# A fused attention and two-layer kernel: four buffers for the even batches' m, and other half-blocks for its four parts

## The chip, the cores and the metric

One NeuronCore of one Trainium2 chip. The metric is the device time of one execution in microseconds (us), over several runs. Matmuls run on the tensor engine (PE), elementwise work on VectorE (DVE), ScalarE (ACT) and GpSimd (POOL); the transfers are issued from SyncE's queue (SP).

## The reference, cut to what matters

```python
# x: [8, 8, 512, 64], state: [8, 8, 32, 64]; heads are joined to 512 columns
a = softmax(x @ state.T / 8)          # each of 512 tokens over 32 states
xread = a @ state
a2 = softmax(state @ x.T / 8)         # each state over 512 tokens
sread = a2 @ x
x = concat([xread, sread])            # 8 batches of 544 tokens, 512 wide
h = relu(x @ w_in)                    # 1024 wide
c = conv3(h)                          # three taps along the tokens, per column
y = (h * sigmoid(c)) @ w_out
xk = mu_k * y + (1 - mu_k) * previous(y)
xr = mu_r * y + (1 - mu_r) * previous(y)
out = sigmoid(xr @ w_r) * (relu(xk @ w_k) ** 2 @ w_v)
```

## The kernel before, in words

Everything runs in float32, with each operand of a large product split into a high and a low part (`fp32r`), and three matmuls (high by high, high by low, low by high) in the place of one (`mm3`).

The first phase works through nine tiles t: t = 0 to 7 are the 512 tokens of batch t, t = 8 the states of all batches. Each tile has eight steps f of 128 hidden columns. A step computes `hps` (the hidden columns before the relu), `hb` (after it), `cacc` (the convolution: one ACT and two DVE instructions), `g` (sigmoid on ACT, product on DVE), `gs` (split into high and low), and `acc`, twelve matmuls of 512 columns with w_out. The second phase does the last three lines of the reference for nine tiles of 512 tokens.

For the tokens the hidden layer isn't computed from xread. The state is multiplied with w_in first: m = state @ w_in, and then `hps` = m.T @ a, six matmuls a step (three for each group g of four heads). m has four parts q for each batch; part q serves the steps f = 2q and 2q + 1. For batches 2 to 7 the products for an even batch and the odd one behind it are made together by `pair_m(b, q, g)`: six matmuls of 256 columns for each of two head groups into one PSUM bank, an eviction (high part on ACT, low part on DVE), and eight transfers for a part, four of which go into the even batch's tile `me` and four into the odd one's `m_odd`. `m_odd` has room for four parts, `me` for two: part q goes into buffer q % 2.

The attention of the next batch is computed beside a batch's steps: scores `p_s`, maxima, exp (`e2`, `q`), norms and transpositions (`aT`, then the split copy `aring` that `hps` reads), transpositions on PE (`p_a2`, copied to `a2T`), the products `p_sr` with x, and their transpositions `p_srT`. Scores, `p_m`, `p_a2`, `p_sr` and `p_srT` share a ring of two PSUM banks (tag "at"). A bank is handed on in the order of the code, when its last reader is done.

What stands where is set in half-blocks: each step f of a tile has two, and batch b begins at half-block 16 b. `M_PARTS` gives for each part the half-block, counted from the batch's first, in which it is emitted; its second head group follows one half-block later. Each emission also has a priority, and a scheduler sets from priorities and readiness the order in which each engine gets its instructions. That order is fixed in the built program: each engine and the SP queue take their instructions strictly in turn.

Of the kernel before, what the change touches and what calls it, by code (L numbers as in the profile page):

```python
# [8 lines left out]
F32 = mybir.dt.float32  # L9
F32R = mybir.dt.float32r  # L10
# [16 lines left out]

ATTEND = 3
M_PARTS = (-8, -4, 3, 8)


@with_exitstack
def tile_kernel(
# [27 lines left out]
    B, P, NST, H, D = x_n.shape  # L61
    KC, S = x_t.shape[1], x_t.shape[3]
    NS = st_bd.shape[2] // (2 * KC)
    KF = w_in.shape[0]
    DM = H * D
    G = H * NS // P
# [117 lines left out]
    def load_s(b, ap):  # L184
        sT[b] = ap.tile([P, KC, 2, NS], F32, tag="sT", name="sT", bufs=3)
        nc.sync.dma_start(out=sT[b].rearrange("p c u n -> p (c u n)"), in_=st_bd[b])

    def load_t(b, ap):
        xT[b] = ap.tile([P, KC, S], F32, tag="xT", name="xT", bufs=1)
        for c in range(KC):  # L190
            nc.sync.dma_start(out=xT[b][:, c], in_=x_t[b, c])

    def load_n(b, ap):
        xn[b] = ap.tile([P, NST, H, D], F32, tag="xn", name="xn", bufs=1)
        nc.sync.dma_start(out=xn[b], in_=x_n[b])

    def m_of(b, q):

        if b % 2:
            return m_odd[:, q]  # L200
        if not m_even:
            m_even.extend(ap.tile([P, 2, G, 2 * P], F32R, tag=f"me{i}", name=f"me{i}") for i in range(2))
        return m_even[q % 2]

    def pair_state(b):

        bd = bds[:, (b // 2 + 1) % 2]
        for i in range(2):
            sb = sT[b + i].rearrange("p c u n -> p c (u n)")
            n = slice(2 * NS * i, 2 * NS * (i + 1))  # L210
            nc.scalar.activation(bd[:, 0, :, n], sb, AF.Copy)
            nc.gpsimd.tensor_tensor(bd[:, 1, :, n], sb, bd[:, 0, :, n].bitcast(F32), op=ALU.subtract)

    def pair_m(b, q, g):

        bd, w = bds[:, (b // 2 + 1) % 2], W["in", "group", q // 2]
        fs = slice(q % 2 * 2, q % 2 * 2 + 2)  # L220
        p = ps_a.tile([P, 512], F32, tag="at", name="p_m")
        for i in range(2):
            c = 2 * g + i
            o = p[:, 2 * P * i:2 * P * (i + 1)].rearrange("p (f c) -> p f c", c=P)
            mm3(o, [(bd[:, 0, c], bd[:, 1, c])], [[w[:, l, fs, c * P:(c + 1) * P] for l in range(2)]], True, True)
        tag = ("raw", "mid")[g]
        r = stg.tile([P, 2, 2, 2 * P], F32R, tag=tag, name="m", bufs=STAGED[tag])
        src = p.rearrange("p (i n) -> p i n", i=2)
        nc.scalar.activation(r[:, 0], src, AF.Copy)
        nc.vector.tensor_tensor(r[:, 1], src, r[:, 0].bitcast(F32), op=ALU.subtract)  # L230
        for j, rj in HALF:
            for i, ri in HALF:
                nc.sync.dma_start(out=m_of(b + j, q)[ri, :, g].bitcast(F32), in_=r[rj, :, i].bitcast(F32))

    class Attention:
# [20 lines left out]
        def m(self, q, f0, n):  # L256

            w = W["in", "group", q // 2]
            fs = slice(q % 2 * 2 + f0, q % 2 * 2 + f0 + n)
            sl = slice(f0 * P, (f0 + n) * P)  # L260
            p = self.at("p_m").rearrange("p (g f c) -> p g f c", g=G, c=P)[:, :, :n]
            for g in range(G):
                cs = (2 * g, 2 * g + 1)
                mm3(
                    p[:, g], [(self.bd[:, 0, c], self.bd[:, 1, c]) for c in cs],
                    [[w[:, l, fs, c * P:(c + 1) * P] for l in range(2)] for c in cs], True, True,
                )
            src = p.rearrange("p g f c -> p g (f c)")
            if self.b == 0:
                nc.scalar.activation(m_first[q // 2][:, q % 2, :, sl], src, AF.Copy)  # L270
                return
            d = m_of(self.b, q)
            nc.scalar.activation(d[:, 0, :, sl], src, AF.Copy)
            nc.vector.tensor_tensor(d[:, 1, :, sl], src, d[:, 0, :, sl].bitcast(F32), op=ALU.subtract)
# [134 lines left out]
    def g1_main(t, f):  # L409
        p = ps_h.tile([P, 512], F32, tag="h", name="hps")  # L410
        if t < B:
            sl = slice(f % 2 * P, f % 2 * P + P)
            if t == 0:
                m = m_first[f // 4][:, f // 2 % 2]
                for g in range(G):
                    nc.tensor.matmul(p, m[:, g, sl], a_first[:, g], start=g == 0, stop=g == G - 1)
                st1[t, f] = {"p": p}
                return
            m, a = m_of(t, f // 2), aring[:, t % 2]
            mm3(  # L420
                p, [(m[:, 0, g, sl], m[:, 1, g, sl]) for g in range(G)],
                [(a[:, 0, g], a[:, 1, g]) for g in range(G)], True, True,
            )
        else:
            v = xs.rearrange("p l c b n -> p l c (b n)")
            mm3(
                p[:, :B * NS], [up(W["in", f], k) for k in range(KC)],
                [(v[:, 0, k], v[:, 1, k]) for k in range(KC)], True, True,
            )
        st1[t, f] = {"p": p}  # L430
# [177 lines left out]
    ap = ap_cm.__enter__()  # L608

    m_first = [ap.tile([P, 2, G, 2 * P], F32, tag=f"me{i}", name=f"mf{i}") for i in range(2)]  # L610
    a_first = ap.tile([P, G, S], F32, tag="af", name="a_first")
    m_even = []
    half = {}

    def at_half(k, *fns, prio=None):
        p = 500 * k - AHEAD if prio is None else prio
        half.setdefault(k, []).extend((fn, p) for fn in fns)
# [51 lines left out]
    def attend(b, k, first):  # L669

        a_ = a if first else Attention(b, ap)
        if not first:
            at_half(k, a_.begin, a_.scores)
            if b == 1:
                at_half(M_PARTS[0] + 2 * KF - 1, a_.state)
            at_half(k + 1, lambda: a_.max1(0, nc.vector), lambda: a_.max1(1, nc.gpsimd))
            at_half(k + 2, lambda: a_.max2(0), lambda: a_.max2(1), a_.neg2)
            at_half(k + 3, a_.exps, prio=500 * k - EXP_AHEAD)
            if b + 1 < B:
                at_half(k + 3, lambda: load_t(b + 1, ap))  # L680
            if b % 2 and b + 1 < B:
                at_half(k + 3, lambda: load_s(b + 1, ap), lambda: load_s(b + 2, ap))
            h = 2 * KF * b
            for q, d in enumerate(M_PARTS):
                if b == 1:
                    at_half(h + d, lambda q=q: a_.m(q, 0, 2), prio=500 * (h + d) - M_AHEAD)
                elif b % 2 == 0:
                    if q == 0:
                        at_half(h + d - 1, lambda: pair_state(b))
                    for g in range(G):  # L690
                        at_half(h + d + g, lambda q=q, g=g: pair_m(b, q, g), prio=500 * (h + d + g) - M_AHEAD)
            at_half(k + 4, lambda: a_.norm1(0, nc.vector))
            at_half(k + 5, lambda: a_.norm1(1, nc.gpsimd))
            at_half(k + 6, lambda: a_.turn1(0))
            at_half(k + 7, lambda: a_.turn1(1))
            k += 9
        at_half(k, a_.norm2, lambda: a_.turn2(0))
        at_half(k + 1, lambda: a_.turn2(1))
        at_half(k + 2, a_.sread)
        if b + 1 < B:  # L700
            at_half(k + 2, lambda: load_n(b + 1, ap))
        at_half(k + 3, a_.sturn)
# [15 lines left out]
    at_half(0, lambda: load_s(1, ap), lambda: load_t(1, ap), prio=-500)  # L718
    at_half(0, lambda: load_n(0, ap), prio=0)
    attend(0, 1, True)  # L720
    for b in range(1, B):
        attend(b, (b - 1) * H1 + ATTEND, False)
# [6 lines left out]
    for i in range(len(slots) + 2):  # L729
        if i < len(slots):  # L730
            ph, t, f = slots[i]
# [98 lines left out]
```

## Time and profile before

| | |
|---|---|
| median of 3 runs | 889.49 us (888.82 to 893.3) |
| profiled execution | 893.46 us, its span 891.6 us |
| PE busy | 853.2 us (96%), 4394 matmuls |
| DVE busy | 546.2 us (61%) |
| ACT busy | 545.1 us (61%) |
| POOL busy | 107.7 us (12%) |

Shares of busy time are means over phases: the first phase fills roughly 80 to 440 us and keeps PE, DVE and ACT busy together, the second is PE's. Matmuls overlap in the pipeline, so the busy time of one (some 0.39 us for 512 columns) is longer than the distance between two.

### The profile page before, as it was taken

The numbers are of one execution on the slowest core, as the hardware profiler recorded it, in microseconds if no ns is written. First come the engines' busy times: TensorE is split into PE (matmuls) and PEld (weight loads), VectorE is DVE, ScalarE is ACT, GpSimd is POOL, SyncE is SP. The second block draws the span as 40 slices with busy tenths as digits, with TensorE's granted clock in tenths as the row PEclk, the third lists the DMA queues.
The fourth block names the chain that finished last, engine by engine and source line by source line (L and its number), as shares of the span: only waits on it lengthen the run. The fifth ranks groups of instructions, "written<-read, shape, count | busy, mean of one in ns | idle before, by whom it ended". The sixth has DMA issues, their size and how long they took to land.

```text
span 891.6 us, 11814 instructions
## 1 busy us (share of the span) xinstructions
PE 853.2 (96%) x4394; PEld 684.5 (77%) x4394; DVE 546.2 (61%) x904; ACT 545.1 (61%) x948; POOL 107.7 (12%) x215
## 2 busy tenths in 40 slices
PE   3879999999999997999999999999999999999997
PEld 1447787678768875889988888888888888888886
DVE  6789987699879979999754352425324253332221
ACT  6677675587568658788866555636455374543431
POOL 2134453332101111211000000000000000000000
PEclk8988999999999998999999999999999999999999
DMA  7450245416344445324311100111101111011010
GB/s 264 163 217 8 106 117 183 122 54 190 118 120 141 117 142 165 132 78 159 120 20 64 48 37 11 48 48 47 48 1 48 47 48 48 2 36 47 1 48 35
DMA packets 45512, 76.85 MB, mean 86 GB/s; under 512 B 8336, under 2 KB 30352, under 8 KB 43408
## 3 DMA queue, kind: packets, MB, share of 16 engines
q1 hardware_dynamic: 45456, 76.12, 26.2%
q8 instruction: 34, 0.56, 0.3%
q14 instruction: 22, 0.18, 0.1%
HBM read 45.66 MB, written 17.86 MB: 71 GB/s over the span
## 4 chain that ended last, share of the span: by engine, by line
PE 84%; DVE 5%; ACT 4%; DMA 4%; issue 1%; SPq 1%; DVEq 0%; ACTq 0%
PE acc L114 13%; PE acc L115 13%; PE acc L116 13%; PE kps L114 7%; PE kps L115 7%; PE kps L116 7%; PE rps L116 3%; PE rps L115 3%; PE rps L114 3%; PE hps L114 3%; PE hps L116 3%; PE hps L115 3%; PE p_s L283 2%; DMA me<-m 1%; PE p_m L114 1%
## 5 line engine op out<-in xcount | busy, mean ns | idle before, releaser
L580 DVE TENSOR_TENSOR ks<-k,ks 128x512 fp32r<-128x512 f32 (+1 forms) x72 | 47.7, 662 | 120.3 <-ACT ks L579 119.8
L115 PE MATMUL kps<-xk,k 128*128 128x512 f32 (+1 forms) x288 | 110.1, 382 | 0.0
L114 PE MATMUL kps<-xk,k 128*128 128x512 f32 (+1 forms) x288 | 110.1, 383 | 0.0
L115 PE MATMUL acc<-gs,out 128*128 128x512 f32 (+1 forms) x288 | 110.1, 384 | 0.0
L116 PE MATMUL kps<-xk,k 128*128 128x512 f32 (+1 forms) x288 | 109.9, 382 | 0.0
L116 PE MATMUL acc<-gs,out 128*128 128x512 f32 (+1 forms) x288 | 109.1, 381 | 0.0
L114 PE MATMUL acc<-v,ks 128*128 128x512 f32 x272 | 106.5, 392 | 0.0
L115 PE MATMUL acc<-v,ks 128*128 128x512 f32 x272 | 105.9, 389 | 0.0
L116 PE MATMUL acc<-v,ks 128*128 128x512 f32 x272 | 105.8, 392 | 0.0
L456 DVE SCALAR_TENSOR_TENSOR cacc<-hb,vcol,cacc 128x512 f32<-128x512 f32 (+1 forms) x138 | 101.4, 745 | 3.4 <-ACT cacc L454 2.7
L114 PE MATMUL acc<-gs,out 128*128 128x512 f32 (+1 forms) x288 | 95.1, 387 | 6.5 <-ACT gs L471 6.5
L545 DVE SCALAR_TENSOR_TENSOR mix<-yt,muc,mix 128x384 f32<-128x384 f32 (+7 forms) x128 | 61.2, 500 | 48.3 <-ACT mix L543 47.6
L579 ACT ACTIVATE ks<-k 128x512 fp32r<-128x512 f32 (+1 forms) x72 | 43.6, 605 | 72.2 <-PE acc L116 72.1
L543 ACT ACTIVATE mix<-yt,om 128x384 f32<-128x384 f32 (+7 forms) x128 | 61.4, 516 | 33.4 <-DMA yt<-y 19.2
L566 ACT ACTIVATE k<-kps 128x512 f32<-128x512 f32 (+1 forms) x72 | 41.0, 569 | 47.4 <-PE kps L116 47.1
L114 PEld LDWEIGHTS acc<-gs,out 128*128 128x128 f32 x288 | 53.5, 190 | 19.5 <-ACT gs L471 8.2
L115 PEld LDWEIGHTS acc<-gs,out 128*128 128x128 f32 x288 | 54.2, 188 | 13.9 <-issue 2.8
L116 PEld LDWEIGHTS acc<-gs,out 128*128 128x128 f32 x288 | 54.2, 188 | 11.5 <-issue 1.9
L551 DVE TENSOR_TENSOR xr<-mix,xr 128x512 fp32r<-128x512 f32 (+1 forms) x36 | 23.8, 662 | 63.4 <-ACT xr L550 63.3
L115 PEld LDWEIGHTS kps<-xk,k 128*128 128x128 f32 x288 | 54.4, 189 | 10.2
L116 PEld LDWEIGHTS kps<-xk,k 128*128 128x128 f32 x288 | 54.3, 188 | 10.1
L114 PEld LDWEIGHTS kps<-xk,k 128*128 128x128 f32 x288 | 54.1, 188 | 10.1
(133 smaller groups left out, 1762.7 us busy)
## 6 DMA issues: line engine op xcount, KB each, us to landing
out<-r SPq DMA_DIRECT2D x34, 256.0 KB, 2.0
xT<-x_t SPq DMA_DIRECT2D x32, 256.0 KB, 4.2
xn<-x_n SPq DMA_DIRECT2D x8, 1024.0 KB, 4.8
y<-yo SPq DMA_DIRECT2D x8, 1024.0 KB, 4.6
me<-m SPq DMA_DIRECT2D x48, 128.0 KB, 2.4
m_odd<-m SPq DMA_DIRECT2D x48, 128.0 KB, 2.4
raw<-w_in SPq DMA_DIRECT2D x8, 512.0 KB, 4.2
raw<-w_out SPq DMA_DIRECT2D x8, 512.0 KB, 5.3
```

What stands on the lines that cost most here:

```text
L114: nc.tensor.matmul(ps, lh, rh, start=start and k == 0, stop=False)
L115: nc.tensor.matmul(ps, lh, rl, start=False, stop=False)
L116: nc.tensor.matmul(ps, ll, rh, start=False, stop=stop and k == last)
L283: nc.tensor.matmul(self.v["s", g][NS * j:NS * (j + 1), :], sT[self.b][r, h // 2, h % 2], xT[self.b][r, h // 2], start=True, stop=True,)
L456: nc.vector.scalar_tensor_tensor(a[:, :n], hb[:, k:k + n], w[k], a[:, :n], op0=ALU.mult, op1=ALU.add)
L543: nc.scalar.activation(tmp[:, o:o + m], y[:, c, q - 1:q - 1 + m], AF.Copy, scale=om[:, i:i + 1])
L545: nc.vector.scalar_tensor_tensor(tmp[:, o:o + m], y[:, c, q:q + m], muc[:, i:i + 1], tmp[:, o:o + m], op0=ALU.mult, op1=ALU.add,)
L551: nc.vector.tensor_tensor(dst[t][:, 1, c, :n], tmp[:, :n], hi.bitcast(F32), op=ALU.subtract)
L566: nc.scalar.activation(k[:, :n], s["p"][:, :n], AF.Relu)
L579: nc.scalar.activation(ks[:, 0, :n], s["k2"][:, :n], AF.Copy)
L580: nc.vector.tensor_tensor(ks[:, 1, :n], s["k2"][:, :n], ks[:, 0, :n].bitcast(F32), op=ALU.subtract)
```

## The change

Even batches get four buffers for m, one for each part. The first batch's `a_first`, which had a place of its own, shares the third one's, so the attention's memory grows by one buffer. And the parts of the pairs are emitted in other half-blocks: the second head group of each still follows one half-block later. The first odd batch, whose m is made alone, keeps the old ones.

```diff
+M_PAIR_PARTS = (-9, -7, 0, 7)
...
-            m_even.extend(ap.tile([P, 2, G, 2 * P], F32R, tag=f"me{i}", name=f"me{i}") for i in range(2))
-        return m_even[q % 2]
+            m_even.extend(ap.tile([P, 2, G, 2 * P], F32R, tag=f"me{i}", name=f"me{i}") for i in range(KF // 2))
+        return m_even[q]
...
-    a_first = ap.tile([P, G, S], F32, tag="af", name="a_first")
+    a_first = ap.tile([P, G, S], F32, tag="me2", name="a_first")
...
-            for q, d in enumerate(M_PARTS):
+            for q, d in enumerate(M_PARTS if b == 1 else M_PAIR_PARTS):
```

The scheduler makes other orders of it. Line numbers of the changed kernel are one higher. On PE, at the end of the pair of batches 2 and 3, the kernel before has the last product of part 3 (second head group), a transposition of batch 3, the second halves of the relu matmuls `hps` of f = 4 and 5 (buffer `me0`), another transposition and `p_sr`, and then the first matmul of f = 6 (buffer `me1`):

```order
L116 MATMUL p_m_1501<-in4_305,aux_103 128x256
L356 MATMUL p_a2_1579<-ident_96,e2_1421 128x128 x4
L114 MATMUL hps_1450<-aring_102,me0_1006 128x512
L115 MATMUL hps_1450<-aring_102,me0_1006 128x512
L116 MATMUL hps_1450<-aring_102,me0_1006 128x512
L114 MATMUL hps_1519<-aring_102,me0_1006 128x512
L115 MATMUL hps_1519<-aring_102,me0_1006 128x512
L116 MATMUL hps_1519<-aring_102,me0_1006 128x512
L356 MATMUL p_a2_1598<-ident_96,e2_1423 128x128 x4
L365 MATMUL p_sr_1626<-xn_1218,a2T_1584 32x64 x16
L114 MATMUL hps_1556<-aring_102,me1_1007 128x512
```

In the changed kernel both head groups of part 3 stand together there (the row shown first is the last of twelve), f = 4 and 5 are done before them, and f = 6 reads the buffer `me3`:

```order
L117 MATMUL p_m_1487<-in4_305,aux_103 128x256
L117 MATMUL acc3_1385<-gs_1528,out2_436 128x512
L357 MATMUL p_a2_1581<-ident_96,e2_1423 128x128 x4
L357 MATMUL p_a2_1600<-ident_96,e2_1425 128x128 x4
L366 MATMUL p_sr_1628<-xn_1220,a2T_1586 32x64 x16
L115 MATMUL hps_1558<-aring_102,me3_969 128x512
L116 MATMUL hps_1558<-aring_102,me3_969 128x512
L117 MATMUL hps_1558<-aring_102,me3_969 128x512
```

From the scores of batch 3 to that first transposition the changed kernel's PE has 33 matmuls of 512 columns (7 `hps`, 26 `acc`) and part 3. At the ends of the two later pairs, twelve `acc` matmuls of f = 3 stand between part 3 and the first transposition, and the `acc` matmuls of f = 4 around the second, before f = 6.

On DVE, before, the evictions of m at the end of the pair 2 and 3 (`m<-p_m`: part 2's second group, and part 3's two) stand behind the transpositions `aT` of batch 3:

```order
L335 TENSOR_TENSOR q_1325<-q_1325,s1_1326 128x512
L342 STREAM_TRANSPOSE aT_1515<-q_1325 128x512
L342 STREAM_TRANSPOSE aT_1540<-q_1325 128x512
L230 TENSOR_TENSOR m_1367<-p_m_1360,m_1367 128x512
L345 TENSOR_TENSOR aring_102<-aT_1515,aring_102 128x512
L230 TENSOR_TENSOR m_1478<-p_m_1471,m_1478 128x512
L345 TENSOR_TENSOR aring_102<-aT_1540,aring_102 128x512
L230 TENSOR_TENSOR m_1508<-p_m_1501,m_1508 128x512
```

In the changed kernel part 2's has moved ahead of the softmax, the convolutions `cacc` of f = 4 and 5 stand in the softmax, and part 3's two evictions behind all of that:

```order
L457 SCALAR_TENSOR_TENSOR cacc_1483<-hb_1479,vcol_97,cacc_1483 128x512
L335 RECIPROCAL s1_1342<-s1_1342 128x16
L336 TENSOR_TENSOR q_1341<-q_1341,s1_1342 128x512
L457 SCALAR_TENSOR_TENSOR cacc_1538<-hb_1534,vcol_97,cacc_1538 128x512
L457 SCALAR_TENSOR_TENSOR cacc_1483<-hb_1479,vcol_97,cacc_1483 128x512
L343 STREAM_TRANSPOSE aT_1517<-q_1341 128x512
L343 STREAM_TRANSPOSE aT_1542<-q_1341 128x512
L231 TENSOR_TENSOR m_1455<-p_m_1448,m_1455 128x512
L457 SCALAR_TENSOR_TENSOR cacc_1538<-hb_1534,vcol_97,cacc_1538 128x512
L231 TENSOR_TENSOR m_1494<-p_m_1487,m_1494 128x512
```

## Rows read from the trace of the kernel before

**Rows 1.** Stretches (start:end, length, busy us of PE, weight loads, DVE, ACT, POOL, clock).
```profile
160.00:175.00 15.00, 13.28 (x119) 8.93 (x119) 8.43 (x17) 10.68 (x19) 2.49 (x8) 0.89 0.64 176
...
325.00:345.00 20.00, 14.30 (x132) 11.17 (x130) 16.22 (x28) 14.21 (x21) 3.07 (x7) 0.99 0.73 221
345.00:352.00 7.00, 5.70 (x14) 4.50 (x15) 7.00 (x10) 7.00 (x11) 1.17 (x2) 0.53 0.17 68
352.00:420.00 68.00, 67.07 (x373) 59.09 (x372) 65.01 (x104) 54.58 (x98) 13.60 (x30) 1.00 0.34 124
...
450.00:882.00 432.00, 432.00 (x1901) 355.97 (x1900) 157.37 (x272) 216.54 (x399) 0.63 (x6) 1.00 0.11 36
```

**Rows 2.** What PE waited for (us in total, times, longest).
```profile
PE acc L114 <- ACT gs L471: 6.5, 2, 5.6
...
PE hps L114 <- DMA me<-m: 3.3, 3, 1.7
...
PE hps L114 <- ACT hb L438: 0.9, 2, 0.6
```

**Rows 3.** Timeline of PE, pair 2/3 (start, us, instruction, idle time before).
```profile
139.27 0.40 PE L116 MATMUL hps<-aring,me 128*128 128x512 f32 x1
...
147.21 1.06 PE L283 MATMUL p_s<-xT,sT 64*32 64x512 f32 x8
...
157.92 0.28 PE L114 MATMUL p_m<-in,aux 128*128 128x256 f32 x1
...
158.63 0.28 PE L114 MATMUL p_m<-in,aux 128*128 128x256 f32 x1
...
162.81 0.60 PE L356 MATMUL p_a<-ident,e 128*128 128x128 f32 x4
...
165.29 0.65 PE L365 MATMUL p_sr<-xn,a2T 128*32 128x64 f32 x32
...
170.15 0.50 PE L114 MATMUL hps<-aring,me 128*128 128x512 f32 x1 [1.69 <-DMA me<-m]
```

**Rows 4.** Timeline of PE, pairs 4/5 and 6/7.
```profile
254.55 0.47 PE L114 MATMUL hps<-aring,me 128*128 128x512 f32 x1 [0.86 <-DMA me<-m]
...
337.45 0.47 PE L114 MATMUL hps<-aring,me 128*128 128x512 f32 x1 [0.76 <-DMA me<-m]
...
346.30 2.07 PE L114 MATMUL acc<-gs,out 128*128 128x512 f32 x4 [5.56 <-ACT gs L471]
```

**Rows 5.** Timeline of the SP queue, pair 2/3: issues of part 3's second group.
```profile
165.49 1.25 SPq L233 DMA_DIRECT2D me<-m  x2
```

**Rows 6.** Transfers into the tile me, all 48.
```profile
DMA to landing us min/median/max: 2.3/2.4/4.0
```

**Rows 7.** Timeline of DVE, pair 2/3.
```profile
149.68 0.70 DVE L304 STREAM_TRANSPOSE q<-p_s 128x512 f32<-128x512 f32 x1
...
157.80 0.71 DVE L342 STREAM_TRANSPOSE aT<-q 128x512 f32<-128x512 f32 x1
...
160.67 0.68 DVE L230 TENSOR_TENSOR m<-p_m,m 128x512 fp32r<-128x512 f32 x1
...
166.28 2.19 DVE L456 SCALAR_TENSOR_TENSOR cacc<-hb,vcol,cacc 128x512 f32<-128x512 f32 x3
```

**Rows 8.** Timeline of ACT, pair 2/3, and last row pair 6/7.
```profile
147.96 1.28 ACT L314 ACT_TABLE_LOAD   x1
152.26 0.69 ACT L314 ACTIVATE e<-p_s,s 128x512 f32<-128x512 f32 x1 [3.02 <-DVE s L300]
...
153.60 1.15 ACT L324 ACTIVATE q<-q,s 128x1024 f32<-128x1024 f32 x1
...
164.26 1.30 ACT L438 ACTIVATE hb<-hps 128x512 f32<-128x512 f32 x2
165.46 0.71 ACT L454 ACTIVATE cacc<-hb,vcol 128x512 f32<-128x512 f32 x1
...
343.59 1.12 ACT L154 ACTIVATE mid<-raw 128x1024 f32<-128x1024 f32 x1
```

## The prediction, made before the changed kernel ran

> **What bounds the kernel now.** I read the table of stretches first. From 450 us on the tensor engine (PE) has no idle time and sends off 1901 matmuls in 432 us, 0.227 us for one [rows 1]; nothing that the change touches stands there. So the change can only move what PE loses in the attention stage before 450 us, and PE loses something in few places there. The list of PE's waits names three waits for the copies of m into `me`, 3.3 us, two waits for a relu (`hb`), 0.9 us, and two for `gs`, 6.5 us, of which one is 5.6 [rows 2]. The timeline puts them at the end of each pair of batches, at what I call places 1, 2 and 3 (pairs 2/3, 4/5, 6/7). Place 1: 1.69 us until a copy has landed [rows 3]. Place 2: 0.86 us. Place 3: 0.6 for `hb`, 0.76 for a copy, and then 5.56 until `gs` of f = 4 is there [rows 4].
>
> PE also loses clock after two of them. In 160 to 175 us the granted clock is 0.89: at the lower of its two levels (1.2 GHz instead of 2.4) for 22% of 15 us, 3.3 us, of which half is lost, 1.6 us. In 345 to 352 it is 0.53: 6.6 us at the low level, 1.3 of them idle, so half of 5.3 is lost, 2.6 us [rows 1]. With that, place 1 costs 3.3 us today, place 2 0.9, place 3 0.6 + 0.76 + 5.56 + 2.6 = 9.5. Together 13.7 us, 1.5% of the run: more than that the change can't give back.
>
> **Room.** The change doubles the buffers of the even batches' m. Did the copies wait for room? At place 1 the late copy goes into the buffer of part 1, whose last reader, the relu matmuls of f = 3, starts its last matmul at 139.27; the copy is issued at 165.49 [rows 3, 5]. The buffer was free for 26 us. The copy is late because part 3's second product comes late on PE (just ahead of the transposition at 162.81 [rows 3]) and then goes through ScalarE (ACT), VectorE (DVE) and a queue (SP) that takes 1.25 us for two issues, with 2.3 to 4.0 us to landing [rows 5, 6]. So the room costs and gives nothing by itself; nothing is added to any engine either (the same products, evictions and copies). What counts is where the parts now stand in each engine's order.
>
> The Trainium skill (Perfetto Trace Analysis, Optimization Strategy) says that a bubble which repeats on the engine that should be saturated can mean that SBUF or PSUM is too small for the next tile. By that rule all 13.7 us could go with the new room; the 26 us above speak against it.
>
> **Part 2** moves ahead of the second batch's scores. Its second product now has about 9 us of other PE work ahead of its reader (29 acc matmuls at 0.227, scores, six relu matmuls); the longest way from product to reader at place 1, from 162.81 to 170.15 at most, is 7.3 us [rows 3]. No wait left there, and the relu products of f = 4 and 5 are done one group of twelve acc matmuls sooner. That is what helps place 3, where `gs` of f = 4 was the long wait. What it pushes back is the scores of the second batch: they follow part 2 in the ring of two PSUM banks, and come some 6 us of PE work later than today at place 1 (18 acc and five relu matmuls, 5.2 us, and half a part, 0.7). With them goes all DVE work of that softmax, and part 3's eviction stands behind it.
>
> **Part 3** is now made in one piece, twelve products of 256 columns, 1.4 us (six in 0.71 [rows 3]).
>
> Place 1, counted from E, the end of the scores (today 147.21 + 1.06 = 148.27 [rows 3]). PE from E to the first transposition `p_a2`: 33 matmuls of 512 columns (7.5 us) and part 3, E+8.9. The way to the free bank: DVE transposes, reduces twice and scales (149.68 to 152.26 today, 2.6 with one foreign 0.6 instruction in it [rows 7, 8]), E+2.1; ACT's two exps and `q` (152.26 to 154.75 [rows 8]), E+4.6; two relus, 1.2, and the first `cacc`, 0.7 [rows 8], E+6.5; then on DVE, ahead of part 3: a `cacc`, the norm, two more `cacc` (0.7 each, three in 2.19), two transpositions (0.65 each) and the eviction itself (0.68) [rows 7], 4.9 with the norm's 0.65 and a reciprocal's 0.2: E+11.4. `p_a2` follows part 3 with only one matmul between and needs its bank: PE waits 2.5 us. Then the copy: two issues 1.25 and 2.4 to landing [rows 5, 6], E+15.1, while PE has 0.9 of transpositions and 0.6 of `p_sr` left (0.60 and 0.65 are their rows, overlapped [rows 3]), E+10.4. Sum of PE's idle time: 4.7 us. The last quarter of m, two pairs of issues later, lands at about E+17.6 by the same rows, when PE comes for it. With an idle time between today's 1.7 (1.6 us of clock lost) and 5.6 (2.6 lost) I take 2.1 for the clock. Place 1: 6.8 against 3.3, a **loss of 3.5**.
>
> Place 2: twelve acc matmuls (2.7 us) and a half group of the next f now stand between part 3 and its users. The softmax is later still: the order puts a relu and the load of the exp table (1.28 us [rows 8]) ahead of the exps, and another table load ahead of part 3's eviction. Added from the same rows: first relu E+2.2 to 2.8, table 4.1, exps 5.4, relu and `cacc` 6.6, `q` 7.7, `gs` 8.3, `cacc` 9.0, table 10.3, sigmoid 10.9, eviction on ACT 11.5, on DVE 12.2. PE reaches its `p_a2` at E+11.5, waits 0.7; 0.2 and 0.6 more for the low halves of `gs` of f = 3 and 4, which DVE makes between. The copy lands at 12.2 + 3.7 = E+15.9, when PE arrives (E+16). 1.5 against 0.9, a **loss of 0.6**; no clock lost, as today.
>
> Place 3: the same as place 2, with the weight splits of the next phase in the queues: ACT has two instructions of about 1.1 [rows 8] right behind `gs` of f = 4, so that what follows is 2.3 later, and I let PE wait all of it. 3.8 against 9.5, a **gain of 5.7**. Can it be kept? In 352 to 420 us DVE is busy 65.0 of 68 us [rows 1], so PE can't run ahead of it by much. But DVE's own idle time of 3.8 us in 325 to 345 (16.2 busy of 20) is filled by the new order, and 3.0 are left behind: 6.8, just enough. If only the 3.8 count, the gain is 3.8.
>
> **Sum:** +3.5 + 0.6 - 5.7 = -1.6 us. The profiled execution took 893.46 us, so it would take 891.9; it is 4.0 above the median of the runs shown, 889.49, and I carry the difference over: **887.9 us**, no change that can be told. About 0.5%, 4.45 us, is what a measurement of this kernel can tell from no change (its three runs lie within 4.5 us).
>
> **Rivals.** (a) Faster: the eviction at place 1 isn't late. For it: all of the 4.7 us rests on the order of DVE, and if DVE gets to part 3 before 2.5 us of that work, place 1 costs no more than today. Against it: the order is fixed when the program is built, and each row ahead has a known length. Time: 887.9 - 3.5 = 884.4, and 882.8 if its clock isn't lost either. (b) Faster by room, a mechanism of its own: the buffers were what the copies and the scheduler waited for, and with four of them all 13.7 us go: 889.5 - 13.7 = 875.8. (This is what the page's rule would make of it.) The 26 us speak against it; only the 5.6 at place 3 speaks for it, as far as it is a result of late copies. (c) Slower: part 3's eviction is late at all three places. At places 2 and 3 the copy lands by my sum just when PE arrives, with no slack, so each us of delay in the softmax is a us of PE. 3.1 us more at both, that is the eviction's end at E+15.3 in place of 12.2, makes +6.2 - 1.6 = +4.6, from where it shows; if both cost what place 1 does (6.8, and 2.3 at place 3) the sum is 3.5 + 5.9 - 0.4 = +9.0: 898.5. For it: DVE is the fuller at place 3, 16.2 of 20 us against 8.4 of 15 at place 1 [rows 1]. Against it: no PE order at places 2 and 3 puts `p_a2` directly behind part 3. (d) The change doesn't do what it says, since room was not the limit and the new half-blocks only shift the same work: 889.5, inside the forecast.
>
> **Numbers.** No change (the sum, its smaller gain at place 3, and d) 0.50, by itself 885 to 894. Faster by over 0.5%: 0.30, of which (b) 0.05 and the rest (a), with the smaller losses at place 2 and 3 that it would bring. Slower: 0.20, (c). The range reaches from 881, which takes in (a) and leaves out (b), to 895.5, which takes in the lower half of (c); about 0.1 lies beyond either end.
>
> **What would show it.** At place 1, PE's first `p_a2` of batch 3 waits 2 to 3 us for DVE's eviction of part 3, and the relu matmuls of f = 6 for the copy; in all 4 to 5.5 us and a granted clock below 0.9 over 15 us there. At place 2 no wait over 1 us. At place 3 the 5.56 us wait for `gs` is gone and the clock stays near 1. Relu matmuls of f = 4 wait for no copy in any pair. From 450 us on all is as before, only shifted. I am wrong if place 1 shows less than 2 us, or if place 3 keeps a wait over 3 us.

## The result, and the profile after

The changed kernel takes 899.15 us in the median of six runs (895.89 to 900.21), the kernel before 889.55 beside it (888.52 to 893.3): ratio 1.0104, 95% interval 1.0084 to 1.0123. It is slower by 1.0%, 9.6 us, where 887.9 us with a range of 881.0 to 895.5 had been forecast. Its profiled execution took 899.27 us, the span is 897.3 us. One profile of the runs below, that of the kernel before again, was taken in a disturbed execution and isn't read.

The list of PE's waits in the changed kernel (us in total, times, longest), which answers to [rows 2]:

```profile
PE acc L115 <- ACT gs L472: 7.2, 3, 3.7
...
PE p_a L357 <- DVE m L231: 3.0, 2, 2.4
...
PE hps L115 <- DMA me<-m: 2.4, 4, 0.9
PE acc L116 <- DVE gs L474: 1.1, 2, 0.7
```

The longest wait at place 3 (5.56 us) is gone, the waits for the copies are shorter, and a wait that the kernel before didn't have stands there: the transposition `p_a2` for the eviction of m. But the sum for `gs` is larger than before, in three waits instead of two. The timeline of PE in the changed kernel says where (start, us, instruction, idle time before); it answers to [rows 3, 4]:

```profile
149.26 1.06 PE L284 MATMUL p_s<-xT,sT 64*32 64x512 f32 x8
...
153.47 1.06 PE L284 MATMUL p_s<-xT,sT 64*32 64x512 f32 x8
...
166.11 0.65 PE L357 MATMUL p_a<-ident,e 128*128 128x128 f32 x4 [2.38 <-DVE m L231]
167.37 0.66 PE L357 MATMUL p_a<-ident,e 128*128 128x128 f32 x4 [0.60 <-DVE m L231]
169.24 0.47 PE L115 MATMUL hps<-aring,me 128*128 128x512 f32 x1 [0.63 <-DMA me<-m]
173.57 0.50 PE L115 MATMUL hps<-aring,me 128*128 128x512 f32 x1 [0.93 <-DMA me<-m]
178.69 1.05 PE L284 MATMUL p_s<-xT,sT 64*32 64x512 f32 x4
180.79 1.04 PE L284 MATMUL p_s<-xT,sT 64*32 64x512 f32 x2
182.42 1.04 PE L284 MATMUL p_s<-xT,sT 64*32 64x512 f32 x2
...
334.78 0.50 PE L116 MATMUL acc<-gs,out 128*128 128x512 f32 x1 [0.68 <-DVE gs L474]
344.07 0.47 PE L115 MATMUL hps<-aring,me 128*128 128x512 f32 x1 [0.52 <-DMA me<-m]
354.21 1.20 PE L115 MATMUL acc<-gs,out 128*128 128x512 f32 x4 [1.43 <-ACT gs L472]
366.34 1.77 PE L115 MATMUL acc<-gs,out 128*128 128x512 f32 x4 [3.68 <-ACT gs L472]
409.65 0.79 PE L115 MATMUL acc<-gs,out 128*128 128x272 f32 x4 [2.09 <-ACT gs L472]
```

Place 1 idles 2.38 + 0.60 + 0.63 + 0.93 = 4.54 us, place 3 0.68 + 0.52 + 1.43 = 2.63. New are the waits at 366 and 409 us, 5.8 us together (for `gs` of f = 0 of the last batch and of f = 2 of the tile behind it), and the scores of batch 4, which run as three bursts from 178.69 on, with relu matmuls of the next tile between.

Stretches of the changed kernel (start:end, length, busy us of PE, weight loads, DVE, ACT, POOL, and third from the end the granted clock), to be held against [rows 1]:

```profile
140.00:160.00 20.00, 20.00 (x101) 14.82 (x100) 13.23 (x24) 10.57 (x19) 5.27 (x7) 1.00 0.58 187
160.00:180.00 20.00, 15.45 (x133) 11.27 (x132) 14.83 (x26) 11.96 (x21) 5.76 (x10) 1.00 0.37 106
340.00:360.00 20.00, 18.05 (x138) 14.28 (x137) 19.95 (x31) 15.58 (x24) 3.82 (x9) 1.00 0.53 162
360.00:380.00 20.00, 16.32 (x65) 13.03 (x64) 19.26 (x28) 14.57 (x22) 1.44 (x7) 0.91 0.34 128
400.00:420.00 20.00, 17.91 (x112) 17.10 (x111) 17.63 (x32) 14.46 (x27) 4.39 (x8) 0.91 0.53 198
```

The clock stays at 1.00 at place 1, although PE idles there for 4.5 us, and at place 3. It falls behind the two new waits: 0.91 over 20 us is some 3.5 us at the lower level (3.4 by stretches of half a microsecond), of which half, 1.7 us, is lost, twice.

What takes ACT past 362 us in the changed kernel (timeline of ACT; in brackets the idle time before and what ended it):

```profile
358.59 0.63 ACT L465 ACTIVATE g<-cacc 128x512 f32<-128x512 f32 x1 [0.80 <-DVE cacc L457]
359.25 0.73 ACT L455 ACTIVATE cacc<-hb,vcol 128x512 f32<-128x512 f32 x1
362.13 1.14 ACT L155 ACTIVATE mid<-raw 128x1024 f32<-128x1024 f32 x1 [2.15 <-DMA raw<-w_v]
363.17 1.13 ACT L157 ACTIVATE raw<-raw 128x1024 uint32<-128x1024 uint32 x1
...
365.65 0.64 ACT L472 ACTIVATE gs<-g 128x512 fp32r<-128x512 f32 x1
```

ACT stands 2.15 us at the split of a piece of w_v, whose transfer has not landed. The `gs` that PE waits for is behind it in the fixed order.

### The profile page after: what moved, and what is told of

Same layout as the page of the kernel before. It is cut to its first block, busy times and chain, and to the rows that moved or that the text cites. A ratio compares the mean times of both kernels' runs of the same rounds, so it can differ in the third digit from the quotient of the medians.

```text
span 897.3 us, 11795 instructions
## 1 busy us (share of the span) xinstructions
PE 856.0 (95%) x4394; PEld 684.6 (76%) x4394; DVE 545.2 (61%) x904; ACT 545.1 (61%) x948; POOL 107.6 (12%) x215
## 4 chain that ended last, share of the span: by engine, by line
PE 83%; DVE 6%; DMA 5%; ACT 3%; issue 1%; SPq 1%; DVEq 0%; ACTq 0%
PE acc L115 12%; PE acc L116 12%; PE acc L117 12%; PE kps L115 7%; PE kps L116 7%; PE kps L117 7%; PE rps L117 3%; PE rps L116 3%; PE rps L115 3%; PE hps L115 3%; PE hps L116 3%; PE hps L117 3%; PE p_s L284 2%; DMA raw<-w_out 1%; DVE cacc L457 1%
## 5 line engine op out<-in xcount | busy, mean ns | idle before, releaser
L457 DVE SCALAR_TENSOR_TENSOR cacc<-hb,vcol,cacc 128x512 f32<-128x512 f32 (+1 forms) x138 | 104.1, 770 | 12.6 <-ACT cacc L455 12.1
L117 PEld LDWEIGHTS acc<-gs,out 128*128 128x128 f32 x288 | 54.2, 188 | 11.6 <-issue 1.9
```

The lines of the kernel that those rows point to most:

```text
L117: nc.tensor.matmul(ps, ll, rh, start=False, stop=stop and k == last)
L457: nc.vector.scalar_tensor_tensor(a[:, :n], hb[:, k:k + n], w[k], a[:, :n], op0=ALU.mult, op1=ALU.add)
```

## A trace to compare with

The kernel before varies by several us from run to run (886.8 to 894.3 over all the groups of runs), and the profiled execution shown above was one of its long ones. The kernel `room_only` (next section) has the same instructions in the same order on every engine, and its profiled execution took 889.37 us, the usual time. Its rows, timeline of PE and three stretches:

```profile
168.89 0.50 PE L115 MATMUL hps<-aring,me 128*128 128x512 f32 x1 [1.85 <-DMA me<-m]
...
330.34 0.50 PE L115 MATMUL hps<-aring,me 128*128 128x512 f32 x1 [0.60 <-ACT hb L439]
333.46 0.47 PE L115 MATMUL hps<-aring,me 128*128 128x512 f32 x1 [0.87 <-DMA me<-m]
342.31 2.07 PE L115 MATMUL acc<-gs,out 128*128 128x512 f32 x4 [5.57 <-ACT gs L472]
414.73 0.79 PE L115 MATMUL acc<-gs,out 128*128 128x272 f32 x4 [0.97 <-ACT gs L472]
```

```profile
140.00:160.00 20.00, 20.00 (x101) 14.88 (x100) 15.45 (x30) 10.16 (x18) 6.88 (x7) 1.00 0.43 138
160.00:180.00 20.00, 18.09 (x150) 12.75 (x149) 14.26 (x26) 13.78 (x24) 6.20 (x13) 1.00 0.49 132
340.00:360.00 20.00, 17.69 (x70) 14.48 (x71) 18.98 (x26) 16.73 (x25) 2.86 (x8) 0.85 0.27 98
```

So in this trace the cost is 1.85 us at place 1, without the clock's 1.6, nothing at place 2, and 0.60 + 0.87 + 5.57 = 7.0 at place 3. The clock is at its lower level there for 6.8 us (339.4 to 346.2), of which PE idles 2.9 (until 342.3): half of 3.9, 1.9, is lost. With 1.85 + 8.9 = 10.8 us the three places hold less than the 13.7 of the prediction. The wait at place 1 is itself no fixed amount: in the eight traces with this order there (the kernel before, `room_only`, and `new_at_3`, `new_at_23`, `old_vr`, `new_at_3_vr`, `early_at_3_vr` and `new_23_vr` of the next section) it is 0.1 to 2.2 us, and the clock falls there in the first alone.

From the last eviction of the first tile's output to the first issue of the result's second tile (108.56 to 537.60 us in the changed kernel, 108.06 to 527.86 here), the changed kernel takes 429.04 us and this one 419.80: +9.2. PE idles 13.74 of it against 10.03 (+3.7), the scores take 12.7 against 10.3 (+2.4), and the clock loses 3.4 against 1.9 (+1.5). The rest, 1.6 us of PE's busy time, I can't place.

## The experiments

Times are medians; behind them stands the ratio to the kernel before, run beside them, with its 95% interval. All kernels but the first have four buffers.

**The kernel before again, and room alone.** The first is the unchanged kernel. The second is the changed one with the old half-blocks:

```diff
-            for q, d in enumerate(M_PARTS if b == 1 else M_PAIR_PARTS):
+            for q, d in enumerate(M_PARTS):
```

> The kernel before, unchanged, for a second profile: the first lay at 893.46 us, 4.0 above the median of 889.5. Theory: the 4 us lie in single waits in the attention stage (places 1 and 3), which differ from run to run, so a profile near 889.5 shows place 3's 5.56 us wait for gs shorter, or place 1's clock whole. Rival: the 4 us are spread over all stages (start, transfers, the phase from 450 us on), and places 1 and 3 look as in the first profile. Time 889.5 by both; a ratio of 1.000 within 0.003 to the kernel before.

> Four buffers for the even batches' m and the first batch's attention in the third of them, but the parts stay in their old half-blocks; each engine then runs the same instructions in the same order as before. Theory (room gives and costs nothing by itself): 889.5 us, ratio 0.998 to 1.002, the same waits at places 1 to 3. Rival (the copies waited for buffers, the rule on consistent bubbles): the waits of hps for the copies of m and the 5.56 us for gs go, 876 to 882 us.

888.92 us, 0.9989 (0.9971 to 1.0007), and 889.46 us, 1.0000 (0.9984 to 1.0016). The first leaves open where the 4 us lay, for want of a profile. The trace of the second shows it as far as one trace can: with the same order, place 1 keeps its clock, place 2 doesn't wait, and the first tile ends 1.4 us earlier (108.06 against 109.49). Place 3 is as in the first profile, where the theory had looked for part of the 4 us. Room gives and costs nothing. The rule of the Trainium skill (Perfetto Trace Analysis, Optimization Strategy), that repeated bubbles can mean too little SBUF or PSUM, would, read as the prediction's rival (b) reads it, have had all of the places' time go with the new room; the time is the same.

**Which place.** The new half-blocks for some pairs only; the others keep the old ones:

```diff
-            for q, d in enumerate(M_PARTS if b == 1 else M_PAIR_PARTS):
+            for q, d in enumerate(M_PAIR_PARTS if b in (2, 4) else M_PARTS):   # new_at_12
+            for q, d in enumerate(M_PAIR_PARTS if b == 6 else M_PARTS):        # new_at_3
+            for q, d in enumerate(M_PAIR_PARTS if b == 2 else M_PARTS):        # new_at_1
+            for q, d in enumerate(M_PAIR_PARTS if b in (4, 6) else M_PARTS):   # new_at_23
```

> The new half-blocks for the parts of batches 2/3 and 4/5 alone; batches 6/7 keep the old ones, with four buffers. Theory A (each place keeps its own account; the loss of the changed kernel is 1.0 at place 1, about 2 for the scores of batch 4 that are split into bursts, -0.2 at place 2, and behind place 3 the queue of ScalarE is blocked): before + 2.8, 892.3 us, with place 3's 5.56 us wait back and no wait over 1.5 us behind it. Rival B (what is lost at places 1 and 2 delays everything by more than their own waits show, and place 3 gains nothing): 897 to 899, as the changed kernel.

> The new half-blocks for the parts of batches 6/7 alone; batches 2/3 and 4/5 keep the old ones, with four buffers. Theory A: -6.9 at place 3, and +5.5 and +3.0 for the two waits for gs behind it (at 366 and 409 us in the changed kernel's trace), since ScalarE has the split of w_v, whose transfer is issued 14 us later, ahead of gs: 889.5 + 1.6 = 891.1 us, both waits there. Rival B (the loss comes from places 1 and 2 and behind them): the two late waits are not there, 882 to 884 us.

> The new half-blocks for batches 2/3 alone (place 1), four buffers. By the traces so far: place 1 idles 4.3 to 4.5 us in the new order and 1.2 to 2.2 in the old one, +2.6; the scores of batch 4 run in three bursts, +2.1 us of PE time; 889.6 + 4.7 = 894.3 us. Rival: some of the 7.7 us that batches 2/3 and 4/5 cost together is only at place 2, and the split burst is paid back by a shorter wait, 891 to 892.

> The new half-blocks for batches 4/5 and 6/7 (places 2 and 3), the old ones for 2/3, four buffers. Theory K (place 1 carries all of the loss): 888.6, as with batches 6/7 alone, + 0.7 for place 2, 889.3 us. Rival L (place 2 costs several us too, by its own wait or by what it shifts behind it): 893 or more.

897.39 us, 1.0080 (1.0055 to 1.0105); 888.59, 0.9987 (0.9971 to 1.0002); 900.60, 1.0123 (1.0104 to 1.0142); 889.52, 1.0002 (0.9986 to 1.0019). The first two ruled out theory A as it stood: the places don't add up from the waits that stand at them (892.3 had been expected of `new_at_12`). `new_at_1` missed both its forecasts, 894.3 and 891 to 892; `new_at_23` came out as theory K had it. Batches 2/3 alone lose all that the change loses (1.0123 against 1.0104, within the intervals); batches 4 to 7 alone lose nothing that can be told.

With batches 6/7 alone the late waits are there too, at 359 and 402 us (timeline of PE of `new_at_3`):

```profile
347.44 1.20 PE L115 MATMUL acc<-gs,out 128*128 128x512 f32 x4 [1.47 <-ACT gs L472]
359.14 1.20 PE L115 MATMUL acc<-gs,out 128*128 128x512 f32 x4 [3.24 <-ACT gs L472]
402.22 0.79 PE L115 MATMUL acc<-gs,out 128*128 128x272 f32 x4 [1.85 <-ACT gs L472]
```

So place 3 gives its gain back by itself, whatever happens at place 1. And with batches 2/3 alone, whose later pairs have the old numbers, places 2 and 3 have longer waits for copies than the kernel before (timeline of PE of `new_at_1`):

```profile
165.87 0.66 PE L357 MATMUL p_a<-ident,e 128*128 128x128 f32 x4 [2.38 <-DVE m L231]
...
258.68 0.47 PE L115 MATMUL hps<-aring,me 128*128 128x512 f32 x1 [2.13 <-DMA me<-m]
...
345.69 0.67 PE L115 MATMUL hps<-aring,me 128*128 128x512 f32 x1 [5.00 <-DMA me<-m]
350.22 0.51 PE L115 MATMUL hps<-aring,m_odd 128*128 128x512 f32 x1 [1.51 <-ACT hb L439]
362.98 2.07 PE L115 MATMUL acc<-gs,out 128*128 128x512 f32 x4 [2.55 <-ACT gs L472]
```

The waits at place 3 come to 9.1 us, where `room_only` has 7.0: the one for `gs` is shorter (2.55 against 5.57), those for the copy and for `hb` longer. Over the same stretch as above (first tile's output to the result's second tile) this kernel takes 430.73 us, 10.9 more than `room_only`: 6.4 of it is idle time of PE, 2.8 at place 1, 2.1 at place 2 and 2.0 at place 3 less 0.7 behind them, 2.1 are the scores' bursts, 1.2 clock, and 1.3 I can't place.

The scheduler sets all later orders from what comes before, so a move at place 1 moves instructions at places 2 and 3 too.

**Which part.**

```diff
-M_PAIR_PARTS = (-9, -7, 0, 7)
+M_PAIR_PARTS = (-9, -7, 3, 8)   # p01_only
+M_PAIR_PARTS = (-9, -7, -4, -1) # p3_early; in early_at_1 for b == 2 alone, else M_PARTS
+M_PAIR_PARTS = (-8, -4, 2, 8)   # p2_at_2, for b == 2 alone, else M_PARTS
```

> Parts 0 and 1 alone in their new half-blocks (-9, -7), parts 2 and 3 as before (3, 8), four buffers, all three pairs. With part 3's number back at 8 and part 2's at 0 the instruction orders are those of the changed kernel, so part 3's own move does nothing and this run shows what is left when part 2 stays. Theory E (all of the change lies in part 2, ahead of the second batch's scores): 889.5 us, PE's waits at places 1 to 3 as before, 1.9, 0 to 0.9, and 0.6 + 0.9 + 5.6 us, no wait for the eviction of m by VectorE. Rival F (the earlier parts 0 and 1 push the rows of the turn of the tile back): 892 or more.

> All four parts ahead of the second batch's scores at all three places, (-9, -7, -4, -1), which four buffers allow; the transpositions then don't stand behind a part in the ring of two PSUM banks. Theory G (what is lost at place 1 is the wait of the first transposition for part 3's bank, whose eviction stands in VectorE's order behind the softmax): no wait of a transposition for the eviction of m, place 1 below 2 us, and 894 us or less. Rival H (what is lost is the scores' later start: each part ahead of them puts off the softmax and all behind it): the wait comes back under another name (the transposition for the exponentials, the relu matmuls for the next aring), 899 or more.

> Batches 2/3 alone changed, with all four parts ahead of the second batch's scores (-9, -7, -4, -1); the others in the old half-blocks. Theory G (place 1 loses by the wait for part 3's bank; without it PE idles there for less than 0.5 us): 889.7 - 1.9 = 887.8 us. Rival M (whatever moves at place 1 gives places 2 and 3 another order, and that is where the time goes): 893 or more, with waits over 2 us at places 2 or 3 that the kernel before doesn't have.

> Batches 2/3 alone changed: only part 2 moves, one half-block earlier (from 3 to 2), which puts its second half ahead of the second batch's scores; parts 0, 1 and 3 and the other pairs as before, four buffers. In PE's order the first transposition then stands 11 rows behind part 3 (in the changed kernel right behind it), and batch 4's scores are in one piece. Theory N (what costs is that the second batch's scores, and so its softmax, come later; the wait moves to wherever PE next needs them): 895 us or more, with waits over 2 us at places 2 or 3 that the kernel before lacks. Rival P (what costs is the wait for part 3's bank and the split scores, and neither is here): 888 to 891.

890.07 us, 1.0009 (0.9988 to 1.0029): parts 0 and 1 cost nothing that can be told, and part 3's number changes no order in the built program, so what costs is part 2's move. 908.67 us, 1.0210 (1.0191 to 1.0230), and 898.39, 1.0094 (1.0076 to 1.0112): without any wait for part 3's bank, and with PE idle for at most 0.4 us from 110 to 200 us in either, these lose as much as the change or more. Theory G falls. Rivals H and M had the right side. Of H's sign a part is there: in `p3_early` transpositions wait 1.22 and 0.89 us for the exponentials at places 2 and 3, and PE 5.42, 3.71 and 3.84 us for `gs` behind them. Of M's sign, waits over 2 us at places 2 or 3 that the kernel before lacks, nothing is there. The waits come later (timeline of PE of `early_at_1`):

```profile
207.67 1.20 PE L116 MATMUL acc<-gs,out 128*128 128x512 f32 x4 [2.04 <-ACT gs L473]
210.19 0.50 PE L117 MATMUL acc<-gs,out 128*128 128x512 f32 x1 [0.61 <-DVE gs L475]
247.88 0.38 PE L116 MATMUL p_m<-in,aux 128*128 128x256 f32 x1 [1.71 <-DVE m L232]
250.97 0.70 PE L116 MATMUL hps<-aring,me 128*128 128x512 f32 x1 [1.65 <-DMA me<-m]
```

The last kernel moves one part of one pair by one half-block, and takes 898.91 us, 1.0094 (1.0066 to 1.0121; the kernel before took 892.05 beside it, 1.0077 by the two medians). Theory N had its number, but not quite its way: of waits over 2 us only one is new, 4.81 us for a copy at place 3 (before: 0.87), while the wait for `gs` there is shorter (2.22 against 5.57). More of the time is clock, 0.91, 0.74 and 0.91 in three stretches, and the scores of batch 4 were split once, which I hadn't expected. Nor is the wait for part 3's bank away: both head groups of part 3 stand in one piece here too, and the first transposition waits 1.44 us behind them, the second 0.60 (2.38 and 0.60 in the changed kernel). So this run doesn't part theory N from rival P; only the runs with part 3 ahead of the scores do. Timeline of PE and stretches of `p2_at_2`:

```profile
165.46 0.66 PE L358 MATMUL p_a<-ident,e 128*128 128x128 f32 x4 [1.44 <-DVE m L232]
```

```profile
140.00:160.00 20.00, 20.00 (x98) 14.70 (x97) 12.30 (x26) 11.04 (x20) 5.70 (x9) 1.00 0.51 165
160.00:180.00 20.00, 17.94 (x140) 13.12 (x139) 14.76 (x25) 11.84 (x21) 5.66 (x10) 0.91 0.37 106
340.00:360.00 20.00, 15.06 (x50) 11.26 (x50) 14.80 (x23) 14.62 (x20) 1.58 (x7) 0.74 0.44 143
360.00:380.00 20.00, 19.16 (x76) 15.36 (x77) 19.97 (x29) 17.18 (x28) 5.45 (x10) 0.91 0.31 110
```

**The split scores.** Batch 4's scores (in `unsplit` batch 6's too) get a slightly more urgent priority:

```diff
-            at_half(k, a_.begin, a_.scores)
+            at_half(k, a_.begin, a_.scores, prio=500 * k - AHEAD - (500 if b in (4, 6) else 0))
```

> The changed kernel, with the scores of batches 4 and 6 a little more urgent, so that the four matmuls of batch 4's first half run in one piece and not in three with relu matmuls between. Theory: the three bursts took 1.05, 1.04 and 1.04 us where one takes 1.06, so 2.1 us of PE time go and the time is 897.1 us; PE's busy time falls by 2. Rival: PE is ahead of its suppliers there, and the 2 us become waits: 899.

> The new half-blocks for batches 2/3 alone, with batch 4's scores a little more urgent, so that they run in one piece. Rival P: the split's 2.1 us go and the wait of 2.4 + 0.6 us for part 3's bank stays; the places behind are as in the kernel before, 889.6 + 2.6 = 892.2 us. Theory N: the 2.1 us of PE time are filled with waiting, 897 to 901 us.

900.12 us, 1.0124 (1.0094 to 1.0154), and 897.06, 1.0057 (1.0037 to 1.0078; before 892.05 beside it). In both the scores of batch 4 run in bursts of 1.06 us again. In the first the orders behind changed as well: at place 2 the transposition now stands behind part 3, as at place 1, and waits 2.35 us for its eviction, and 1.11 for the copy `a2T` on ACT, and at 370 us PE waits 6.22 us for `gs`; the kernel gains nothing, against both forecasts' 897 to 899. In the second, by the ratio, some 5.8 us go of the 10.9 that batches 2/3 cost, more than the 2.1 of the bursts; by the time alone 3.5. Both forecasts miss by the ratio (5.1 us over the kernel before, where 2.6 and at least 7 had been expected), though 897.06 itself lies in theory N's range. It doesn't settle how much is the split's.

**The splits of the weights.** They are put behind a `gs` in ACT's order (in `v_later` only that of w_v, in the changed kernel); `gsi` holds, for each tile and step, the instruction that makes the high part of `gs`:

```diff
+    def behind(w, key):
+        def split():
+            with tc.issue_after(gsi[key].ins):
+                w[1]()
+        return w[0], split
...
                     w = weight(w_v, "v", "wa", wp, k, 2, 4)
+                    if k == 0:
+                        w = behind(w, (B - 1, 1))
...
                     w = weight(w_r, "r", "wb", wp, k, 2, 2)
+                    w = behind(w, (B, 3 + k // 2))
```

> The changed kernel, with the split of the first piece of w_v put behind gs of f = 1 of the last batch in ScalarE's order (it stood ahead of gs of f = 0, and waited 2.15 us for its transfer there). Theory C (PE's 3.68 us wait for gs at 366 us and the 1.8 us of clock behind it come from ScalarE's order): that wait goes below 1 us and the clock of 360 to 380 us is 1.00, 899.2 - 5.5 = 893.7 us; the wait of 2.09 us at 409 stays. Rival D (DVE, busy 19.95 of 20 us just ahead of it, is the bound there): a wait of the same length comes back for a low half of gs or another product of DVE, 897 to 899.

> New half-blocks for batches 6/7 alone, the split of the first w_v behind gs of f = 1 of the last batch, and the two splits of w_r behind gs of f = 3 and 4 of the last tile of the first phase. Theory C: of the 888.6 us with the new half-blocks for batches 6/7 alone the waits of 3.24 and 1.85 us for gs and 1.7 us of clock go, 881.8 us, faster than the kernel before by 0.9%. Rival D (DVE is the bound behind place 3, or the splits that are put off delay the next phase): 887 to 890.

> The parts in their old half-blocks with four buffers, and only the splits of the first w_v and of w_r put off as in the faster kernel. Theory I (place 3's 5.56 us wait for gs is the earlier bound there, and the order of the splits helps only when it is gone): the 5.56 us wait stays, 889 to 890.5 us. Rival J (the order of the splits is all of the gain of 3.9 us): 885.5 to 886.5.

> Batches 6/7 alone with all four parts ahead of the second batch's scores, and the splits of w_v and w_r put off. Theory G (the later a part, the later gs of f = 4 and 6): the waits of 0.67 for a copy of m and 1.32 us for gs at place 3 go as well, 885.9 - 2 = 884 us. Rival H (the scores of the last batch start later, and everything behind them): 888 to 891.

> The new half-blocks at places 2 and 3, the old ones at place 1, and the splits of w_v and w_r put off. Theory K: 885.9 + 0.7 = 886.6 us. Rival L: 889 or more.

> The three moves that gave something, together: batches 2/3 with all parts ahead of the scores, 4/5 as before, 6/7 in the new half-blocks, and the splits of w_v and w_r put off. Theory G: 885.9 us less the 1.4 that place 1 idled there, 884.4 us. Rival M: 888 or more.

`v_later`: 897.20 us, 1.0090 (1.0061 to 1.0119). The 3.68 us wait becomes 1.27 and the clock of 360 to 380 us is whole, as theory C had it, but waits of 0.40, 0.53 and 0.57 are new, and the time falls by 2 us, not 5.5: it lies in rival D's 897 to 899, and by the ratios (1.0104 and 1.0090) it can't be told from the changed kernel's. `new_at_3_vr`: 885.86 us, 0.9957 (0.9938 to 0.9975), the lowest median of all, between theory C's 881.8 and rival D's 887 to 890. Its timeline of PE:

```profile
346.32 1.19 PE L115 MATMUL acc<-gs,out 128*128 128x512 f32 x4 [1.32 <-ACT gs L473]
356.04 0.96 PE L115 MATMUL acc<-gs,out 128*128 128x512 f32 x3 [1.27 <-ACT gs L473]
...
391.97 0.53 PE L115 MATMUL acc<-gs,out 128*128 128x272 f32 x2 [0.56 <-ACT gs L473]
```

The 3.24 us of `new_at_3` are down to 1.27; the 1.85 us, which stood at f = 2 of the last tile, are gone, and 0.56 stand at its f = 0. The clock is 1.00 from 300 us on. `old_vr`: 886.94 us, 0.9967 (0.9953 to 0.9981), with the 5.55 us wait still there: the order of the splits gives some 2.9 us without any move of m, against theory I, and the new half-blocks at place 3 add no more than the measurement can tell. DVE in 340 to 400 us, first `old_vr`, then `new_at_3_vr` (start:end, length, busy us of PE, weight loads, DVE, ACT, POOL, clock):

```profile
340.00:400.00 60.00, 57.55 (x288) 49.42 (x289) 57.58 (x91) 48.99 (x86) 12.58 (x31) 0.94 0.31 116
340.00:400.00 60.00, 55.90 (x296) 46.65 (x295) 59.75 (x98) 51.18 (x88) 18.79 (x31) 1.00 0.38 136
```

`early_at_3_vr`: 887.40, 0.9982 (0.9968 to 0.9996), between its two forecasts. `new_23_vr`: 886.83, 0.9971 (0.9957 to 0.9986), as theory K had it. `early_1_new_3_vr`: 896.86, 1.0074 (1.0054 to 1.0093): it differs from `new_at_3_vr` by the move at place 1 alone.

**What the runs have in common.** The ten kernels in which the second half of part 2 stands ahead of batch 3's scores have ratios from 1.0057 to 1.0210; the nine others from 0.9957 to 1.0009. Nothing else that was varied sorts them so.

## Why the prediction was wrong

Between the forecast sum, -1.6 us, and the result, +9.6, lie 11.2 us. Changed alone, batches 2/3 cost 10.9 us where +3.5 had been forecast, and batches 6/7 give 1.1 where -5.7 had been. Two steps failed: the price of putting the second batch's scores back, which the prediction saw under "Part 2" but charged only with the waits at the places themselves, and "Can it be kept?" at place 3.

**Room.** Right: 1.0000 for the buffers alone.

**Place 1.** The walk was right to within 1.4 us, its balance was not. From the end of the scores (153.47 + 1.06 = 154.53) the transposition starts after 11.6 us (forecast 11.4), the relu matmuls after 14.7 (15.1) and 19.0 (17.6); idle 4.54 against 4.7. But the clock was not lost (2.1 forecast). The kernel before loses 1.85 there in `room_only`'s trace (0.1 to 2.2 in others of the same order) and not 3.3, since the 1.6 of clock in the profiled execution were no standing cost. And the three bursts of scores, 2.1 us, were not in the sum. So the place itself loses 2.7 + 2.1 = 4.8 where +3.5 had been forecast.

**Place 2.** 0.68 us in the changed kernel's trace, no wait over 1 us, as listed (1.5 forecast), and no cost that can be told by `new_at_23`.

**Place 3.** The term of -5.7. At the place itself it came: 2.6 us against 8.9, so -6.3. The step that failed is the answer to "Can it be kept?": DVE's 6.8 us of idle time were to make it "just enough". With place 3 alone changed the gain is 1.1 us (0.9987, no difference that can be told), and PE waits 3.24 and 1.85 us for `gs` behind the splits of w_v and w_r. The prediction had the splits in ACT's queue at place 3, but no split that waits for its transfer with `gs` behind it. That these two waits come from the splits' place in ACT's order is shown by `new_at_3_vr`, where the first shrinks to 1.27 and the second goes (0.56 are new two steps ahead of it) when only the splits move. That they are what took the gain is not shown: with the splits put off in both, the new half-blocks at place 3 still bring only 1.1 us (885.86 against `old_vr`'s 886.94, intervals overlapping), and not 5.7. Where they stand so, DVE is busy 59.75 of 60 us from 340 to 400 us (59.74 in `new_23_vr` and `v_later`), against 57.58 in `old_vr`. So the bound may be the one that the prediction named, DVE, with less to spare than the 6.8 us; no run that takes work from DVE there tests it.

**The sum.** Its form failed as well. It took each place by itself and the orders between as given. Batches 2/3 alone cost 10.9 us (1.0123), of which some 4.9 stand at place 1 (2.8 of waits, 2.1 of bursts); most of the rest are waits at places 2 and 3 and clock. And the wait for part 3's bank, on which the walk was built, isn't needed for the loss: `early_at_1` loses 0.9% without it. What is shown is that part 2 ahead of batch 3's scores costs 0.6 to 1.2% in the four kernels that change batches 2/3 and leave the later pairs' numbers. Why it does so at place 1 and not at places 2 and 3 is open. One reason can only be argued: DVE has 28.1 and 27.1 us of work in 140 to 180 us where the scores come late (13.23 + 14.83 in the changed kernel, 12.30 + 14.76 in `p2_at_2`), and 29.7 where they don't (15.45 + 14.26 in `room_only`); what is missing has to be done later, beside the next pair. In the traces of all ten kernels with late scores these 40 us hold 27.1 to 28.8 us of DVE's work, in seven of the others and `room_only` 29.3 to 31.4; the kernel before, in its long execution, has 28.7.

**The rivals.** (a), (b) and (d) fell. (c) named 898.5 us and the right side, but not the way, so that its number is luck: no transposition waits for part 3's eviction at places 2 and 3. From 450 us on everything is only shifted, as said.

## What to carry to other kernels

Where a scheduler fixes the order, a wait that is removed isn't a term that can be summed: look for the next instruction in the supplying engine's queue that waits for a transfer, ask whether another engine there has time to spare, and try the move at one place at a time. Work that is pulled ahead of a long chain (here the scores, and behind them the softmax) can cost more than the waits that show at that spot: 10.9 us at place 1, with about 4.9 there, and nothing that can be told at places 2 and 3. Before a price is read from one profile, hold it against a second profile of the same order: of the 13.7 us that the three places seemed to hold here, 2.9 were not there in the next one.

## What was not expected of the hardware

A burst of score matmuls takes about the same time whether the trace counts two, four or eight in it: 1.04, 1.05 and 1.06 us in the changed kernel. Cut into three, it costs three times as much.

The clock doesn't follow the length of the idle time alone. In the changed kernel 4.54 us in four waits at place 1 left it at 1.00, in `v_later` 3.20 us in three waits of the same order (2.38, 0.60, 0.22) came with 0.91 over 160 to 180 us, and in the kernel before 1.69 in one with 0.89 [rows 1, 3]; `room_only`, with the same order, 1.85 and 1.00.
